# Halves of w_in by model dimension, four early blocks, and batch 1's k and v in halves: one edit to a fused attention and feed-forward kernel

## The chip, the cores and the metric

The kernel runs on one core of a Trainium2 chip. The metric is the time of the whole program on the device in microseconds; runs of one kernel on this chip agree within some tenths of a per cent. One execution was also recorded by the hardware profiler, and all times "at" a point below are counted from the start of that recording. PE is the TensorE (matmul) engine, ACT is ScalarE, DVE is VectorE, POOL is GpSimd and SP is SyncE, which here only issues DMA requests.

## The reference

Linear attention over 8 batches of 8 heads, 576 positions and 64 features, followed by a feed-forward layer with a "snake" activation. Everything is float32 in the reference; the kernel computes its matmuls in bf16.

```python
q_s = softmax(q, axis=features);  k_s = softmax(k, axis=positions)
kv  = einsum('bhsd,bhse->bhde', k_s, v)
x   = einsum('bhsd,bhde->bhse', q_s, kv)      # -> 4608 tokens x 512
h   = x @ w_in                                # 4608 x 2048
g   = h + sin(alpha*h)**2 / (alpha + 1e-9)
out = g @ w_out                               # 4608 x 512
```

## The kernel before

**Tiles.** The tokens are cut into 9 tiles `t` of 512. A batch has 9 blocks of 64 tokens, so tile 0 is the first 8 blocks of batch 0, tile 1 is block 8 of batch 0 and the first 7 blocks of batch 1, and so on. `xT` holds x transposed: 4 chunks of 128 model dimensions (the k steps `ki`) by 4608 tokens.

**The two matmul stages.** For one tile, `mm_h` (L248) makes 16 blocks `ni` of 128 columns of h, each with 4 matmuls, one for each `ki`, accumulated in one PSUM buffer. On each block ACT takes the sine (L254), ACT, POOL or DVE squares it (L256, L258, L260; letters A, P, D in a string say which), and DVE adds the parts to g (`combine`, L264), which frees the block's PSUM buffer. `combine` runs one block behind. The squares live in a pool of 4 `s` buffers. Then `mm_o` (L268) makes the output, 4 row groups `m` by 16 steps over `ni`, and the sums are copied out (L274) and stored (L277). For tile 0 this output stage is `o_quad`, with four accumulators open at once and an order written out by hand: four groups `c` of four w_out rows each, by `m` first or by row first. For later tiles it is `o_stream`, one accumulator after the other.

**Hand-made order.** Every engine runs its instructions in the order in which the code issues them. `take(os, n)` puts the next n output matmuls at that place of PE's order, so attention work of batch 1 is threaded between tile 0's last output matmuls.

**PSUM.** `ps_h` has 4 buffers of one bank; `ps_e` has 2 buffers of two banks, used by the attention steps of batches 0 and 1 and lent to some of the h blocks (`wide`; in the trace these are called `hh`, those in `ps_h` `hp`). Which blocks are lent is decided by `ni % 6`: (2, 3) for tile 0, (4, 5) for tile 1. A new tile of a pool gets the buffer that was released first. After tile 1's h blocks `ps_e` is closed, and `ps_o` (accumulators, called `op`) and `ps_a` take its banks: `ps_o` the first two-bank buffer, `ps_a` the second.

**The head.** Batch 0's q, k, v come in halves; half `ii` holds heads of chunks 2ii and 2ii+1. `kv_mm` (L171) and `kv_norm` (L181, L184) make the block-diagonal `kbd` of a half, `q_transpose_ii` (L200) transposes the normalised q, and `attn_chunk` (L228, `xp`) makes one chunk of x, copied to `xT` (L355, L357, L363). The first two blocks of h do their k steps 0 and 1 ahead of the rest. ACT loads the Sin table (L364) after the last of these copies.

**Requests.** SP asks for q, k, v. POOL asks for w_in (five column ranges, each in two halves by partition) and w_out (four groups of 4 rows): the first eight rows early, the rest by `late`, a table of what is issued after block `ni` of tile 0. `late` also asks for q of batch 1 and, with two small DVE copies as a gate (L90), for k of batch 1. v of batch 1 takes the staging buffer of batch 0's q, which is free after the exp of q's ninth block (block 8).

Of the kernel before, what the change touches and what calls it, by code (L numbers as in the profile page):

```python
# [15 lines left out]
F32 = mybir.dt.float32  # L16
# [7 lines left out]
def kernel(  # L24
# [14 lines left out]
    nc = tc.nc  # L39
# [37 lines left out]
    def src_view(t, b):  # L77
        return t[b].rearrange("(i e) (p j) d -> (e p) i (j d)", e=2, j=J)
# [26 lines left out]
    def load_win(c0, c1):  # L105
        n = slice(c0, c1)
        for x in range(2):
            nc.gpsimd.dma_start(out=win[64 * x:64 * x + 64, :, n], in_=win_v[x][:, :, n])

    def load_wout(c):  # L110
        nc.gpsimd.dma_start(out=wout[:, 4 * c:4 * c + 4, :], in_=wout_v[:, 4 * c:4 * c + 4, :])
# [122 lines left out]
    HP = {}  # L234

    def mm_h(t, ni, wide=None, k0=0, k1=4):

        if ni == 0 and k0 == 0:
            G[t] = gpool.tile([128, nN, MF], BF16, name="g")
        if k0:  # L240
            hp = HP[t, ni]
        elif wide and ni % 6 in ((2, 3) if t == 0 else (4, 5)):
            hp = wide()
        else:
            hp = ps_h.tile([128, MF], F32, name="hp", tag="h")
        HP[t, ni] = hp
        for ki in range(k0, k1):
            nc.tensor.matmul(hp, win[:, ki, ni * 128:(ni + 1) * 128],  # L248
                             xT[:, ki, t * MF:(t + 1) * MF], start=(ki == 0), stop=(ki == 3))
        return hp  # L250
# [70 lines left out]
    for c0, c1 in ((0, 256), (256, 512), (512, 1024), (1024, 1536), (1536, 2048)):  # L321
        load_win(c0, c1)
    for c in range(2):
        load_wout(c)
# [24 lines left out]
    cast_v0(1, 0, 5, ACT_CP)  # L349
    cast_v0(1, 5, 9, DVE_CP)  # L350

# [5 lines left out]
    ACT_CP(xT[:, 1, 0:MF], xp[1])  # L357
    kv_mm(0, 1, ps_e, split=True)
    kv_norm(0, 1, 2)
    xp = [ps_e.tile([128, 2, MF], F32, name="xp", tag="a")[:, 0] for _ in range(2)]  # L360
    for e in range(2):
        attn_chunk(0, 2 + e, 0, 8, xp[e])
        (DVE_CP, ACT_CP)[e](xT[:, 2 + e, 0:MF], xp[e])  # L363
    nc.scalar.activation(zero, zero, AX.Sin)  # L364
    for ki in range(2):
        for ni in range(2):
            mm_h(0, ni, None, ki, ki + 1)

    def h_slot(t, ni, sq, lag, wide=None):
        hp = mm_h(t, ni, wide, 2 if t < 2 and ni < 2 else 0)  # L370
        lag.append((t, ni, hp, sine(t, ni, hp, sq)))
# [5 lines left out]
    def o_quad(t, accs, engs):  # L377

        R = range(4)
        by_m, by_n = [(n, m) for m in R for n in R], [(n, m) for n in R for m in R]  # L380
        orders = [by_m, by_n, by_n, by_m]
        for c in R:
            for n, m in orders[c]:
                mm_o(t, m, 4 * c + n, accs[m])
                if c == 3 and n == 3:
                    evac_o(t, m, accs[m], engs[m])
                yield
# [9 lines left out]
    with ES:  # L397
        def lent():
            return ps_e.tile([128, 2, MF], F32, name="hh", tag="a")[:, 0]

        def load_q8():
            for ii in range(2):
                load0(nc.sync, "q", q, ii, 8, 9)

        def load_q1():
            staged["q", 1] = st = stage.tile([128, 4, J, D], F32, name="st_q", tag="st")
            for ii in range(2):
                DVE_CP(st[:, ii, 0, 0:1], zero)
            for ii in range(2):
                nc.sync.dma_start(out=st[:, ii::2, 0:7].rearrange("p i j d -> p i (j d)"),  # L410
                                  in_=src_view(q, 1)[:, ii::2, 0:7 * D])

        late = {4: load_q8, 6: load_q1, 8: lambda: load_wout(2),
                10: lambda: load_wout(3), 13: lambda: load("k", k, 1, halves=True, gate=DVE_CP)}
# [10 lines left out]
        exp_to(A["qe", 0][:, 8:9], staged["q", 0][:, :, 8:9])  # L425
        for ii in range(2):
            exp_half("q", 1, ii, 7)
        load("v", v, 1, halves=True)
        nc.sync.dma_start(out=q78.rearrange("p i j d -> p i (j d)"), in_=src_view(q, 1)[:, :, 7 * D:J * D])
        load_batch(2)  # L430
        norm_late(0, 8)
        norm_q(1, [GP, V], 7)
        exp_k(1)
# [9 lines left out]
        take(os, 6)  # L443
# [4 lines left out]
        cast_v(1, [ACT_CP, DVE_CP])  # L448
        exp_to(A["qe", 1][:, 7:J], q78)
        take(os, 3)  # L450
        kv_mm(1, 0, ps_e, split=True)
        kv_norm(1, 0, 1)
        take(os, 3)
        kv_mm(1, 1, ps_e, split=True)
        kv_norm(1, 1, 2)
        take(os, 1)

        c0 = J * P
        for ii in range(2):
            xp = ps_e.tile([128, 2, 512], F32, name="xp", tag="a")[:, :, 0:7 * P]  # L460
            for e in range(2):
                attn_chunk(1, 2 * ii + e, 0, 7, xp[:, e])
            (ACT_CP, DVE_CP)[ii](xT[:, 2 * ii:2 * ii + 2, c0:c0 + 7 * P], xp)
            if ii == 0:
                nc.scalar.activation(zero, zero, AX.Sin)
            take(os, 2)
# [5 lines left out]
        for ki in range(2):  # L472
            for ni in range(2):
                mm_h(1, ni, lent, ki, ki + 1)
# [72 lines left out]
    def lent():  # L547
        return ps_o.tile([128, MF], F32, name="op", tag="o")
# [70 lines left out]
```

## Time and profile before

| what | value |
|---|---|
| median of 3 runs | 287.51 us (287.39 to 287.79) |
| span of the profiled execution | 285.8 us; its own time is not given apart from the span |
| PE busy | 272.6 us, 95% of the span |
| ACT, DVE, POOL busy | 226.0, 192.6, 80.6 us |
| granted TensorE clock | 0.999 on the mean |
| first h matmul of tile 0, first output matmul of tile 0 | 14.64 us, 28.42 us |
| first h matmul of tile 1, first output matmul of tile 1 | 46.14 us, 59.95 us |
| batch 1: k halves landed | 37.33 and 39.40 us |
| batch 1: v halves landed | 40.85 and 42.28 us |

The span is from the first to the last instruction; the median of the runs is 1.7 us longer than it. Busy times are unions of an engine's instructions. A matmul of 512 columns is shown as 0.379 us, but a new one starts every 0.216 us, so PE's idle time is read from the starts and not from the ends. In a timeline row the columns are the start, the duration, the engine, the line, the operation, out<-in, the shapes and the count; brackets at the end give the engine's idle time ahead of it and what ended it.

### The profile page before, as it was taken

How to read it: one execution, taken by the hardware profiler on the slowest of the kernel's cores; microseconds unless marked ns; L12 is line 12 of the kernel's file. 1: busy time of each engine (PE TensorE's matmuls, PEld its weight loads, DVE VectorE, ACT ScalarE, POOL GpSimd, SP SyncE). 2: the span in 40 equal slices, each digit the busy share in tenths (PEclk: the TensorE clock that was granted, in tenths of full speed). 3: DMA queues.
4: the chain of work that ended last, by engine and by line, in shares of the span. 5: the costliest groups of instructions: out<-in, count | busy, mean ns of one | idle time of the engine just before them, and what ended most of it. 6: DMA issues, size and time to landing. Idle time of an engine off the chain costs nothing.

```text
span 285.8 us, 4247 instructions
## 1 busy us (share of the span) xinstructions
PE 272.6 (95%) x1541; PEld 130.8 (46%) x1569; DVE 192.6 (67%) x291; ACT 226.0 (79%) x321; POOL 80.6 (28%) x75
## 2 busy tenths in 40 slices
PE   2899999999999999999999999999999999999994
PEld 1444454445454454444544454445444444444443
DVE  4857967999999658766785677667674555555321
ACT  4898748999489999899889988998877777777400
POOL 2869512773477480005300530041000000000000
PEclk9999999999999999999999999999999999999999
DMA  7999999843999984139711990016011111111242
GB/s 261 308 204 243 260 397 407 312 169 78 275 222 412 372 169 105 37 69 406 218 38 39 359 292 20 22 36 155 1 39 37 37 37 39 37 38 41 46 100 73
DMA packets 38581, 45.77 MB, mean 160 GB/s; under 512 B 16528, under 2 KB 22432, under 8 KB 38560
## 3 DMA queue, kind: packets, MB, share of 16 engines
q1 hardware_dynamic: 33376, 40.57, 46.3%
q0 software_dynamic: 4992, 4.79, 9.7%
q8 instruction: 12, 0.20, 0.3%
q10 hardware_dynamic: 192, 0.14, 0.2%
q14 instruction: 9, 0.07, 0.1%
HBM read 36.71 MB, written 9.44 MB: 161 GB/s over the span
## 4 chain that ended last, share of the span: by engine, by line
PE 74%; DVE 9%; DMA 7%; ACT 4%; issue 3%; POOL 2%; SPq 0%; ACTq 0%
PE op L268 33%; PE hp L248 33%; DMA st_v<-in_v_dram 5%; ACT s L254 3%; DVE g L264 2%; POOL s L258 2%; PE kvp L171 2%; DVE qs L150 2%; PE xp L220 2%; DMA st_q<-in_q_dram 1%; PE op L589 1%; PE hh L248 1%; DVE vb L137 1%; DVE qn L152 1%; DVE kbd L184 1%
## 5 line engine op out<-in xcount | busy, mean ns | idle before, releaser
L264 DVE SCALAR_TENSOR_TENSOR g<-s,inva_sb,hp 128x512 bf16<-128x512 f32 x130 | 96.0, 745 | 58.4 <-ACT s L256 54.2
L248 PE MATMUL hp<-xT,win 128*128 128x512 bf16 x512 | 129.0, 379 | 0.5
L268 PE MATMUL op<-wout,g 128*128 128x512 bf16 x479 | 121.9, 379 | 1.2 <-issue 0.6
L254 ACT ACTIVATE s<-hp,alpha_sb 128x512 f32<-128x512 f32 x130 | 87.8, 682 | 25.1 <-PE hp L248 22.6
L248 PEld LDWEIGHTS <-win 128*128 128x128 bf16 x576 | 56.3, 98 | 67.5 <-issue 0.8
L268 PEld LDWEIGHTS <-g 128*128 128x128 bf16 x560 | 54.1, 98 | 61.1 <-issue 0.4
L256 ACT ACTIVATE s<-s 128x512 f32<-128x512 f32 x111 | 69.9, 630 | 3.5
L152 POOL TENSOR_TENSOR qn<-qe,qs 128x1152 bf16<-128x1152 bf16 (+1 forms) x12 | 24.9, 2091 | 78.6 <-DVE qs L146 69.2
L258 POOL TENSOR_TENSOR s<-s 128x512 f32<-128x512 f32 x30 | 33.0, 1111 | 22.3 <-ACT s L254 22.0
L274 DVE COPY o<-op 128x512 f32<-128x512 f32 (+2 forms) x33 | 22.0, 668 | 9.7 <-PE op L268 5.8
L118 ACT ACTIVATE ke<-st_k 128x1152 bf16<-128x1152 f32 x16 | 17.9, 1151 | 5.0 <-DMA st_k<-in_k_dram 5.0
L118 ACT ACTIVATE qe<-st_q 128x1152 bf16<-128x1152 f32 (+3 forms) x18 | 17.7, 1025 | 2.1 <-DMA st_q<-in_q_dram 1.9
L145 DVE TENSOR_REDUCE qs<-qe 128x36 f32<-128x2304 bf16 x5 | 12.8, 2553 | 8.7 <-ACT qe L118 8.6
L268 PE MATMUL hp<-wout,g 128*128 128x512 bf16 x62 | 14.8, 379 | 0.2 <-issue 0.2
L223 DVE CAST xT<-xp 128x512 bf16<-128x512 f32 (+1 forms) x18 | 13.4, 742 | 0.0
L137 POOL CAST vb<-st_v 128x1152 bf16<-128x1152 f32 x10 | 11.3, 1163 | 6.5 <-DMA st_v<-in_v_dram 6.5
L171 PEld LDWEIGHTS <-ke 64*128 64x128 bf16 x288 | 8.4, 93 | 4.9 <-issue 1.9
L171 PE MATMUL kvp<-vb,ke 64*128 64x130 bf16 x288 | 9.9, 216 | 0.7 <-ACT vb L137 0.4
L118 ACT ACT_TABLE_LOAD x7 | 9.0, 1283 | 1.3 <-PEq L603 1.2
L248 PE MATMUL hh<-xT,win 128*128 128x512 bf16 x39 | 9.6, 379 | 0.1
L220 PE MATMUL xp<-qT,kbd 128*128 128x256 bf16 (+1 forms) x40 | 8.2, 286 | 0.4 <-DVE xT L223 0.3
L150 DVE TENSOR_REDUCE qs<-qe 128x16 f32<-128x1024 bf16 (+2 forms) x6 | 7.2, 1197 | 1.8 <-ACT qe L118 1.8
(79 smaller groups left out, 123.1 us busy)
## 6 DMA issues: line engine op xcount, KB each, us to landing
out_dram<-o SPq DMA_DIRECT2D x70, 128.0 KB, 2.3
st_q<-in_q_dram SPq DMA_DIRECT2D x6, 1152.0 KB, 6.7
st_k<-in_k_dram SPq DMA_DIRECT2D x6, 1152.0 KB, 8.9
st_v<-in_v_dram SPq DMA_DIRECT2D x6, 1152.0 KB, 10.2
st_k<-in_k_dram SPq DMA_DIRECT2D x4, 576.0 KB, 7.1
wout<-in_moe_w_out_dram POOLq DMA_DIRECT2D x4, 512.0 KB, 11.7
st_v<-in_v_dram SPq DMA_DIRECT2D x3, 576.0 KB, 9.4
win<-in_moe_w_in_dram POOLq DMA_DIRECT2D x6, 256.0 KB, 7.7
```

What stands on the lines that cost most here:

```text
L118: nc.scalar.activation(dst[:, :, ii * 128:(ii + 1) * 128].rearrange("p j (x d) -> p x j d", x=2), src[:, ii::2], AX.Exp)
L137: engs[ii](vv[:, 2 * ii:2 * ii + 2, :, 0:D], staged["v", b][:, ii::2])
L152: engs[ii % len(engs)].tensor_tensor(qn[:, ii, 0:j1].rearrange("p j (x d) -> p j x d", x=2), qe[:, ii], part.unsqueeze(3).to_broadcast([12 ...
L171: nc.tensor.matmul(kvp[:, e, ii * 130:(ii + 1) * 130], ke[r, j, ii * 128:(ii + 1) * 128], vt[r, j, ii * 130:(ii + 1) * 130], start=(j == 0 ...
L220: nc.tensor.matmul(xp[:, e, 0:n], kt[:, e, ii], qT[:, ii, j0:j1, e * 64:(e + 1) * 64], start=True, stop=True)
L248: nc.tensor.matmul(hp, win[:, ki, ni * 128:(ni + 1) * 128], xT[:, ki, t * MF:(t + 1) * MF], start=(ki == 0), stop=(ki == 3))
L254: nc.scalar.activation(s, hp, AX.Sin, scale=alpha_sb[:, ni:ni + 1])
L256: nc.scalar.activation(s, s, AX.Square)
L258: nc.gpsimd.tensor_tensor(s, s, s, op=ALU.mult)
L264: nc.vector.scalar_tensor_tensor(G[t][:, ni], in0=s, scalar=inva_sb[:, ni:ni + 1], in1=hp, op0=ALU.mult, op1=ALU.add)
L268: nc.tensor.matmul(acc, G[t][:, ni, j * 128:(j + 1) * 128], wout[:, ni, :], start=(ni == 0), stop=(ni == nN - 1))
L274: eng(o[:, cols], acc)
```

## The change

It has these parts:

- **w_in's first columns.** Columns 0 to 511 are asked for in two halves by model dimension (k steps 0-1, then 2-3) and not as two column ranges; the later ranges are 512 columns each as before. The cast of part of v of batch 0 goes from ACT to POOL, between the w_in requests.
- **Four early blocks.** Blocks 0 to 2 of tile 0 do k step 0 ahead of the last two x chunks; block 3 follows behind those, and then all four do k step 1. The Sin table is loaded ahead of this. Both x chunks now share one two-bank buffer.
- **Lent buffers.** The blocks of tile 0 that use `ps_e` are those with `ni % 6` 3 or 5, from block 3 on; in tile 1 those with 0 or 1, where blocks 0 and 1 share one buffer. From tile 2 on the choice is as before.
- **Batch 1.** k and v are asked for together, half by half (k, v, k, v), after block 13 of tile 0, with one DVE copy as a gate. q's ninth block of batch 0 is loaded into `q78` behind batch 1's q. The exps, casts, `kv_mm` and x chunks of batch 1 are issued half by half, and blocks 0 and 1 of tile 1 do k steps 0 and 1 between `kv_mm` of the second half and its x chunks.
- **w_out's last rows.** Rows 12-13 are asked for in `late`, rows 14-15 after the normalisation of batch 1's q. In the last group of `o_quad` rows 12 and 13 go first for all four accumulators, then 14 and 15.

The diff, cut to its core:

```diff
-    def load_win(c0, c1):
-        n = slice(c0, c1)
+    def load_win(c0, c1, k0=0, k1=4):
+        n, kk = slice(c0, c1), slice(k0, k1)
...
+    LENT = {0: (3, 5), 1: (0, 1), 2: (4, 5)}
...
-        elif wide and ni % 6 in ((2, 3) if t == 0 else (4, 5)):
-            hp = wide()
+        elif wide and ni % 6 in LENT[t]:
+            hp = wide(t, ni)
...
-    for c0, c1 in ((0, 256), (256, 512), (512, 1024), (1024, 1536), (1536, 2048)):
-        load_win(c0, c1)
+    load_win(0, 512, 0, 2)
+    load_win(0, 512, 2, 4)
+    load_win(512, 1024)
+    cast_v0(1, 0, 5, GP_CP)
+    for c in range(2, 4):
+        load_win(512 * c, 512 * c + 512)
...
-    cast_v0(1, 0, 5, ACT_CP)
     cast_v0(1, 5, 9, DVE_CP)
+
+    def lent(t, ni):
+        if (t, ni) != (1, 1):
+            HP["pair"] = ps_e.tile([128, 2, MF], F32, name="hh", tag="a")
+        return HP["pair"][:, int((t, ni) == (1, 1))]
...
+    nc.scalar.activation(zero, zero, AX.Sin)
     kv_mm(0, 1, ps_e, split=True)
     kv_norm(0, 1, 2)
-    xp = [ps_e.tile([128, 2, MF], F32, name="xp", tag="a")[:, 0] for _ in range(2)]
+    for ni in range(3):
+        mm_h(0, ni, lent, 0, 1)
+    xp = ps_e.tile([128, 2, MF], F32, name="xp", tag="a")
     for e in range(2):
-        attn_chunk(0, 2 + e, 0, 8, xp[e])
-        (DVE_CP, ACT_CP)[e](xT[:, 2 + e, 0:MF], xp[e])
-    nc.scalar.activation(zero, zero, AX.Sin)
-    for ki in range(2):
-        for ni in range(2):
-            mm_h(0, ni, None, ki, ki + 1)
+        attn_chunk(0, 2 + e, 0, 8, xp[:, e])
+    for e in range(2):
+        (DVE_CP, ACT_CP)[e](xT[:, 2 + e, 0:MF], xp[:, e])
+    mm_h(0, 3, lent, 0, 1)
+    for ni in range(4):
+        mm_h(0, ni, lent, 1, 2)
...
-        orders = [by_m, by_n, by_n, by_m]
+        orders = [by_m, by_n, by_n, by_n[:8] + [(n, m) for m in R for n in (2, 3)]]
...
+            nc.sync.dma_start(out=q78[:, :, 0], in_=src_view(q, 0)[:, :, 8 * D:J * D])
+
+        def load_kv1():
+            for n in "kv":
+                staged[n, 1] = stage.tile([128, 4, J, D], F32, name=f"st_{n}", tag="st")
+            DVE_CP(staged["k", 1][:, 0, 0, 0:1], zero)
+            for ii in range(2):
+                for n, t in (("k", k), ("v", v)):
+                    nc.sync.dma_start(out=staged[n, 1][:, ii::2].rearrange("p i j d -> p i (j d)"),
+                                      in_=src_view(t, 1)[:, ii::2])
-        late = {4: load_q8, 6: load_q1, 8: lambda: load_wout(2),
-                10: lambda: load_wout(3), 13: lambda: load("k", k, 1, halves=True, gate=DVE_CP)}
+        late = {6: load_q1, 8: lambda: load_wout(8, 12), 10: lambda: load_wout(12, 14), 13: load_kv1}
...
-        exp_to(A["qe", 0][:, 8:9], staged["q", 0][:, :, 8:9])
         for ii in range(2):
             exp_half("q", 1, ii, 7)
-        load("v", v, 1, halves=True)
+        exp_to(A["qe", 0][:, 8:9], q78[:, :, 0:1])
...
-        norm_late(0, 8)
         norm_q(1, [GP, V], 7)
-        exp_k(1)
+        norm_late(0, 8)
+        load_wout(14, 16)
...
+        exp_half("k", 1, 0)
+        cast_v1(0, ACT_CP)
+        exp_half("k", 1, 1)
...
-        take(os, 6)
+        take(os, 4)
         xp = ps_e.tile([128, 4, P], F32, name="xp", tag="a")
...
+        kv_mm(1, 0, ps_e, split=True)
+        kv_norm(1, 0, 1)
+        cast_v1(1, DVE_CP)
+        take(os, 4)
+        x_half(0, ACT_CP)
+        exp_to(A["qe", 1][:, 7:J], q78)
+        nc.scalar.activation(zero, zero, AX.Sin)
+        take(os, 2)
+        kv_mm(1, 1, ps_e, split=True)
+        kv_norm(1, 1, 2)
+        for ki in range(2):
+            for ni in range(2):
+                mm_h(1, ni, lent, ki, ki + 1)
+        x_half(1, DVE_CP)
         take(os)
```

`x_half(ii, eng)` makes the two x chunks of a half for 7 blocks of batch 1 and copies them to `xT`, as the loop at L459 did.

## The prediction

> **What bounds the kernel now.** I read the chain that ended last, then TensorE's (PE's) timeline round every edit, then VectorE's (DVE's), then the landings of the requests that move.
>
> ```profile
> PE 74%; DVE 9%; DMA 7%; ACT 4%; issue 3%; POOL 2%; SPq 0%; ACTq 0%
> ```
>
> PE sets the end: sixteen 128x512 matmuls from 46.14 are followed by the next at 49.59, so one costs 0.216 us, and nearly all of the span is such steps. A change is worth what it takes from or adds to PE's idle time; what leaves PE busy at its old place costs nothing.
>
> ```profile
> 11.78 0.60 PE L228 MATMUL hp<-qT,kbd 128*128 128x512 bf16 x2
> 12.39 0.69 PE L171 MATMUL kvp<-vb,ke 64*128 64x130 bf16 x18
> 13.98 0.61 PE L228 MATMUL xp<-qT,kbd 128*128 128x512 bf16 x2 [0.90 <-DVE kbd L184]
> 14.64 1.67 PE L248 MATMUL hp<-xT,win 128*128 128x512 bf16 x7
> 16.15 1.03 PE L248 MATMUL hh<-xT,win 128*128 128x512 bf16 x4
> ```
>
> This is the head (start, duration, count). PE idles 0.90 us for DVE's kbd; from 14.64 it is dense, so the head offers at most that 0.90 and a 0.22 step at 14.43.
>
> ```profile
> 28.42 10.28 PE L268 MATMUL hp<-wout,g 128*128 128x512 bf16 x45
> 38.54 0.95 PE L200 MATMUL tp<-identb,qn 128*128 128x128 bf16 x14
> 40.73 0.28 PE L228 MATMUL xp<-qT,kbd 128*128 128x64 bf16 x4
> 42.09 0.69 PE L171 MATMUL kvp<-vb,ke 64*128 64x130 bf16 x18 [0.44 <-ACT vb L137]
> 42.94 0.59 PE L268 MATMUL hp<-wout,g 128*128 128x512 bf16 x2 [0.16 <-issue]
> 46.14 1.03 PE L248 MATMUL hp<-xT,win 128*128 128x512 bf16 x4
> ```
>
> Here tile 0's output stage starts at 28.42. Its first 46 matmuls (one record is missing) last 10.12 us where 46 x 0.216 = 9.93: 0.19 of waiting is hidden in the group. Batch 1's k and v cost PE 0.44 + 0.16 us of idleness between 41.5 and 43.
>
> ```profile
> 28.55 0.75 DVE L264 SCALAR_TENSOR_TENSOR g<-s,inva_sb,hp 128x512 bf16<-128x512 f32 x1 [0.38 <-POOL s L258]
> 29.54 0.75 DVE L264 SCALAR_TENSOR_TENSOR g<-s,inva_sb,hp 128x512 bf16<-128x512 f32 x1 [0.24 <-POOL s L258]
> 30.33 0.74 DVE L264 SCALAR_TENSOR_TENSOR g<-s,inva_sb,hp 128x512 bf16<-128x512 f32 x1
> 30.98 1.44 DVE L264 SCALAR_TENSOR_TENSOR g<-s,inva_sb,hh 128x512 bf16<-128x512 f32 x2
> ```
>
> These are the `combine` steps of blocks 11, 12, 13 and 14-15 of tile 0, each freeing the PSUM buffer its block was in. The four accumulators of the output stage take over the buffers of the last four blocks in `ps_h`: now blocks 10, 11, 12, 13. PE wants the second accumulator 4 matmuls after 28.42, at 29.28, and block 11's combine ends at 29.30; it wants the third at 30.2 and block 12's ends at 30.29. That is the hidden 0.19.
>
> ```profile
> 58.58 1.39 DVE L264 SCALAR_TENSOR_TENSOR g<-s,inva_sb,hh 128x512 bf16<-128x512 f32 x2
> 59.90 2.15 DVE L264 SCALAR_TENSOR_TENSOR g<-s,inva_sb,hp 128x512 bf16<-128x512 f32 x3
> ```
> ```profile
> 59.95 2.32 PE L268 MATMUL op<-wout,g 128*128 128x512 bf16 x9
> ```
>
> The same handover at the end of tile 1: `ps_o` lies on the first buffer of `ps_e`, last used by block 10 (the first of the two `hh` at 58.58, done 59.31). PE starts at 59.95 without waiting; blocks 12, 13 and 14 are combined from 59.90 on.
>
> **Part 1, the head.** Three k-step-0 matmuls (3 x 0.216 = 0.65 us) move into the idle 13.08 to 13.98. They need xT's first chunk (DVE until 13.11) and the first w_in pair.
>
> ```profile
> L108 POOL DMA_DIRECT2D win<-in_moe_w_in_dram x1: 659/659/659, 8.2 to 8.2; - x1
> DMA to landing us min/median/max: 5.5/5.5/5.5
> ```
>
> This is the pair's second half: issued 8.25, landed 13.75. The changed pair has the same bytes, so 13.80 is one bound for the start; xT's 13.17 is the other. q's ninth block (128 KB, landed 0.46 us behind k at 9.99) leaves the queue ahead, so I take 13.4. Three matmuls to 14.05, two xp (0.43), five more matmuls (1.08) end at 15.56, with one 0.22 step 15.6 to 15.8; from 13.80 it is 15.96 to 16.2. Before, the same eight matmuls ended at 14.64 + 1.73 = 16.37. Lead: 0.2 to 0.8, taken 0.6. Columns 512 to 1024 landed at 17.66 (10.66 + 7.0) and are wanted four half-blocks later, at 17.3 to 17.7: they may eat 0.3 of the lead.
>
> Hidden edits: the cast of v to GpSimd (POOL) takes some 0.65 us (1.16 x 640/1152), ready near 12.05 for kv_mm at 12.39. It stands ahead of four w_in and two w_out issues, queued behind transfers until 17.66 anyway; POOL's first square is wanted at 17.9 and its issues then end near 16.9. Without that cover each late us of the cast delays kv_mm as much. ScalarE (ACT) loses that 0.72 cast; the Sin load comes ahead of xT's last copy, from about 13.4. The load's row takes 1.28 us (15.23) and the next instruction starts 0.01 later: xT's copy then runs 14.9 to 15.5, just before PE wants it. [...]
>
> **Part 2, buffers of tile 0.** Lent blocks become 3, 5, 9, 11, 15, so the last four in `ps_h` are 10, 12, 13, 14 (a pool gives out the buffer released first), and the second accumulator waits for block 12, not 11. Block 12's combine ends at 30.29 now. Its chain (POOL's squares one behind the other, ACT's sines held by four `s` buffers) starts at ACT's first sine, 16.63, held by the Sin load. Then it starts when block 0 is done, 0.64 us after PE's 15.6 to 15.96: up to 0.4 earlier. The second late w_out issue on POOL is halved in descriptors (0.79 to about 0.66, the w_in issues' row): 0.13 more. So the combine ends at 29.75 to 30.2, and the remaining twelve matmuls of the first group end 12 x 0.216 = 2.59 us later, at 32.4 to 32.8. Third and fourth accumulator follow 0.70 us apart, hidden under 0.86 of matmuls. Before, that point was 28.42 + 3.45 + 0.19 = 32.06. The head's lead is gone, and 0.3 to 0.7 more; **+0.5**.
>
> **Part 3, batch 1's k and v.** Asked for together from 30.2 (q's old buffer is free early), they still share the queue with the same bytes: v's halves landed at 40.85 and 42.28, third and fourth; now v's first half is second, at about 39.2. That takes out the 0.60 us of waiting. q's ninth block, now ahead of k, costs that queue the 0.46 us of its old row; the halved w_out request gives as much back. Its exp also holds SyncE until about 34.3, with q78's second part and batch 2 behind it (32.36 before); k and v fill the queue until 42, so nobody waits. In return only 4, not 6, output matmuls cover DVE's three qT copies: transposes at 38.54, last copy ended 40.48, 1.94 later; PE has 0.89 + 0.86 = 1.75 of work, so it waits some 0.3 with the semaphore. The rest is reordered: after each kv_mm, kbd is ready 1.15 us later (43.93 to 45.05), against 4 matmuls, 0.86 plus 0.15 to 0.37 of restart: 0 to 0.2 each. Sum -0.60 + 0.3 + 0.2 x 2 = **+0.1**, between -0.5 (both waits gone, nothing new) and +0.5. The request for w_out's rows 14-15 stands on POOL behind the qn multiply, at about 35.5; nothing queued behind it is wanted before the next sine near 47. Rows 12-15 took 38.60 - 33.72 = 4.9 us once the queue was theirs, so half takes 2.5, plus issue and latency: about 41, wanted near 46. [...]
>
> **Part 4, buffers of tile 1.** Lent blocks become 0, 1, 6, 7, 12, 13. By release order block 12 sits in `ps_e`'s first buffer, so the output stage's first accumulator waits for its combine: 59.90 + 0.73, against PE's 59.95. Relative to PE that chain is unchanged (ACT waits for PE's blocks 11 and 12). The wait is **+0.65**, up to 0.9 if the evacuations and norm_late, which now come later on DVE, push it. Nothing gives it back: DVE's next evacuation (63.83, waiting 0.26 for PE) heads the chain to batch 3's v request at 71.84.
>
> **Sum.** +0.5 + 0.1 + 0.65 = +1.25 us against the profiled span of 285.8; what lies round it (1.7 us to the median 287.51) stays. 287.51 + 1.25 = 288.8, its own range 0.3 - 0.3 + 0.4 to 0.7 + 0.5 + 0.9: 287.9 to 289.6.
>
> **Rivals.** (a) Faster: the buffers bind nothing and PE keeps the head's 0.6 and part 3's 0.6: 287.51 - 1.2 = 286.3. For it: both waits hang on combines that an earlier ACT could advance. Against: block 12's combine would have to end by 29.0, 1.3 us earlier, and POOL is dense from 22.88 on. It decides where that combine ends before the fourth output matmul; chance 0.18. (b) A wash: the lower ends, +0.3, -0.3 and +0.4, with a stronger k and v gain of another 0.2: 287.7; chance 0.14. (c) Rows 14-15 late: if half the rows take 11.9 us like the whole request at 26.66, they land at 47.4 to 48, 1.5 after PE wants them: 288.8 + 1.5 = 290.3. The queue ahead of that request, which is gone here, speaks against; chance 0.07. The forecast has 0.61.
>
> **Numbers.** About 0.2%, 0.57 us, is what a measurement can tell: faster is below 286.9, slower above 288.1. Faster: 0.18 from (a), 0.01 from the forecast's tail. Same: (b) and 0.01. Slower: (c) and the forecast's rest. The range takes the forecast, (b) and the near part of (a): 286.7 to 289.8.
>
> **What would show it.** Right: PE's first L248 near 13.4 and eight matmuls done before 16; a stall of about 0.9 us after four output matmuls near 29, ended by a DVE combine; no wait for vb near 42; a stall of 0.6 before the first `op` of tile 1's output. Wrong: output matmuls dense from the start, or `op` following the last block at once.

## The result and the profile after

The changed kernel takes 290.76 us (median of 4 runs, 290.35 to 291.31) against 287.45 us before: 1.0107 times, 95% interval 1.009 to 1.0125. The direction was forecast, the size was not: 288.8 us was predicted and the range ended at 289.8. The profiled execution has a span of 288.6 us (285.8 before) and a time of its own of 290.35 us, the shortest of the four, so what it shows covers 2.8 of the 3.3 us between the medians. Line numbers after the change are one higher than before (L249 is the h matmul, L269 the output matmul, L255 the sine, L265 `combine`).

The chain that ended last, by engine, in the page of the changed kernel:

```profile
PE 75%; DVE 9%; DMA 6%; POOL 4%; ACT 2%; issue 2%; SPq 0%; ACTq 0%
```

PE still sets the end, so the 2.8 us must be idle time of PE. TensorE's timeline of the changed kernel, round every edit (start, duration, engine, line, operation; in brackets the idle time ahead of it and what ended that):

```profile
13.52 0.81 PE L249 MATMUL hp<-xT,win 128*128 128x512 bf16 x3
14.31 0.60 PE L228 MATMUL xp<-qT,kbd 128*128 128x512 bf16 x2
...
15.83 1.72 PE L249 MATMUL hp<-xT,win 128*128 128x512 bf16 x6
17.39 0.59 PE L249 MATMUL hh<-xT,win 128*128 128x512 bf16 x2
18.35 1.02 PE L249 MATMUL hp<-xT,win 128*128 128x512 bf16 x4 [0.36 <-DMA win<-in_moe_w_in_dram]
...
28.70 1.03 PE L269 MATMUL hp<-wout,g 128*128 128x512 bf16 x4
30.59 9.22 PE L269 MATMUL hp<-wout,g 128*128 128x512 bf16 x42 [0.85 <-DVE g L265]
39.65 0.94 PE L200 MATMUL tp<-identb,qn 128*128 128x128 bf16 x14
...
41.87 0.68 PE L171 MATMUL kvp<-vb,ke 64*128 64x130 bf16 x18
...
44.38 0.69 PE L171 MATMUL kvp<-vb,ke 64*128 64x130 bf16 x18
...
48.09 0.59 PE L249 MATMUL hh<-xT,win 128*128 128x512 bf16 x2
49.84 0.59 PE L249 MATMUL hh<-xT,win 128*128 128x512 bf16 x2 [1.16 <-ACT s L255]
...
63.02 2.32 PE L269 MATMUL op<-wout,g 128*128 128x512 bf16 x10 [0.50 <-DVE g L265]
```

Four places lose time. Block 4 of tile 0 waits for w_in's columns 512 on (18.35). After four output matmuls the second accumulator waits for a combine (30.59). Tile 1's block 1 waits 1.16 us for ACT's sine (49.84), which no step of the prediction had. The first `op` waits for a combine (63.02). In this profile neither `kv_mm` of batch 1 waits (41.87 and 44.38 have no bracket).

The account, from marks that both traces have (us):

| stretch | before | after | difference |
|---|---|---|---|
| start of the span to tile 0's first output matmul | 28.42 | 28.70 | +0.28 |
| from there to batch 1's transposes (46 output matmuls) | 10.12 | 10.95 | +0.83 |
| transposes to tile 1's h, less four early matmuls (4 x 0.216) | 7.60 | 7.58 | -0.02 |
| tile 1's h, 64 matmuls, to the first `op` | 13.81 | 15.79 | +1.98 |
| from there to the end | 225.80 | 225.55 | -0.25 |
| sum | 285.75 | 288.57 | +2.82 |

A step, here and below, is the time from one matmul's start to the next, 0.216 us when nothing waits; the 1.16 and 0.50 us of the brackets are 1.32 and 0.66 us beyond that. They make up the fourth row's 1.98.

The first row is chance as far as these profiles show. The second `kv_mm` of batch 0 started at 12.72 instead of 12.39; `p_before` below, whose head is that of the kernel before, started it at 12.66 and its output at 28.70, as late as the changed kernel. Counted from that `kv_mm`, tile 0's output began after 16.03 us before, 16.04 in `p_before` and 15.98 after the change.

### The profile page after: what moved, and what is told of

Read it like the earlier page. It is cut to its first block, busy times and chain, and to the rows that moved or that the text cites. A ratio compares the mean times of both kernels' runs of the same rounds, so it can differ in the third digit from the quotient of the medians.

```text
span 288.6 us, 4272 instructions
## 1 busy us (share of the span) xinstructions
PE 276.0 (96%) x1569; PEld 130.8 (45%) x1569; DVE 193.4 (67%) x290; ACT 225.9 (78%) x320; POOL 81.2 (28%) x77
## 4 chain that ended last, share of the span: by engine, by line
PE 75%; DVE 9%; DMA 6%; POOL 4%; ACT 2%; issue 2%; SPq 0%; ACTq 0%
PE op L269 34%; PE hp L249 30%; DVE g L265 4%; PE hp L269 4%; DMA win<-in_moe_w_in_dram 3%; DMA st_v<-in_v_dram 2%; ACT s L255 2%; PE kvp L171 2%; POOL s L259 2%; DMA st_k<-in_k_dram 2%; PE xp L220 2%; PE hh L249 1%; PE op L610 1%; DVE vb L137 1%; POOL win L108 1%
## 5 line engine op out<-in xcount | busy, mean ns | idle before, releaser
L265 DVE SCALAR_TENSOR_TENSOR g<-s,inva_sb,hp 128x512 bf16<-128x512 f32 x129 | 95.2, 745 | 57.3 <-ACT s L257 54.2
L249 PE MATMUL hp<-xT,win 128*128 128x512 bf16 x516 | 129.6, 379 | 0.6 <-DMA win<-in_moe_w_in_dram 0.4
L269 PE MATMUL op<-wout,g 128*128 128x512 bf16 x496 | 124.4, 379 | 0.5 <-DVE g L265 0.5
L255 ACT ACTIVATE s<-hp,alpha_sb 128x512 f32<-128x512 f32 x129 | 87.5, 683 | 25.3 <-PE hp L249 24.3
L249 PEld LDWEIGHTS <-win 128*128 128x128 bf16 x576 | 56.0, 98 | 69.5 <-issue 3.2
L269 PEld LDWEIGHTS <-g 128*128 128x128 bf16 x560 | 54.1, 98 | 62.8 <-issue 1.9
L259 POOL TENSOR_TENSOR s<-s 128x512 f32<-128x512 f32 x30 | 32.3, 1089 | 25.5 <-ACT s L255 25.2
L118 ACT ACTIVATE qe<-st_q 128x1152 bf16<-128x1152 f32 (+2 forms) x16 | 17.2, 1115 | 2.3 <-DMA st_q<-in_q_dram 2.1
L269 PE MATMUL hp<-wout,g 128*128 128x512 bf16 x64 | 14.8, 379 | 0.9 <-DVE g L265 0.9
L223 DVE CAST xT<-xp 128x512 bf16<-128x512 f32 (+1 forms) x18 | 13.4, 743 | 0.0
L249 PE MATMUL hh<-xT,win 128*128 128x512 bf16 x44 | 11.4, 379 | 1.2 <-ACT s L255 1.2
L265 DVE SCALAR_TENSOR_TENSOR g<-s,inva_sb,hh 128x512 bf16<-128x512 f32 x11 | 8.0, 742 | 2.1 <-POOL s L259 2.0
L255 ACT ACTIVATE s<-hh,alpha_sb 128x512 f32<-128x512 f32 x11 | 7.4, 682 | 2.0 <-PE hh L249 1.9
```

The lines of the kernel that those rows point to most:

```text
L118: nc.scalar.activation(dst[:, :, ii * 128:(ii + 1) * 128].rearrange("p j (x d) -> p x j d", x=2), src[:, ii::2], AX.Exp)
L223: eng(xT[:, 2 * ii:2 * ii + 2, c0:c0 + n], xp[:, :, 0:n])
L249: nc.tensor.matmul(hp, win[:, ki, ni * 128:(ni + 1) * 128], xT[:, ki, t * MF:(t + 1) * MF], start=(ki == 0), stop=(ki == 3))
L255: nc.scalar.activation(s, hp, AX.Sin, scale=alpha_sb[:, ni:ni + 1])
L259: nc.gpsimd.tensor_tensor(s, s, s, op=ALU.mult)
L265: nc.vector.scalar_tensor_tensor(G[t][:, ni], in0=s, scalar=inva_sb[:, ni:ni + 1], in1=hp, op0=ALU.mult, op1=ALU.add)
```

## The experiments

The first three are the changed kernel with one handover mended each; the fourth is the second with one cast moved back. All later ones use the normalised q of batches 2 to 7 untransposed, by plain copies of the same bytes, so that they have a before and an after of their own (`p_before`, `p_after`); their line numbers are six or more lower than those of the changed kernel. The table gives the stretches of each profile; ratios are to the kernel before, run on the same chip beside it. Four chips were used (e1 to e4; `p_before` to `p_m1`; `p_h1` to `p_f3`; `p_m4` and `p_f4`), so across these groups the ratios compare and the medians do not.

| kernel | median us | ratio, 95% interval | start to first sine | sine to tile 0's output | output to transposes | transposes to tile 1's first sine | sine to `op` | `op` to end |
|---|---|---|---|---|---|---|---|---|
| before | 287.45 | - | 16.63 | 11.79 | 10.12 | 9.16 | 12.26 | 225.80 |
| after | 290.76 | 1.0107 (1.009-1.0125) | 16.73 | 11.97 | 10.95 | 9.46 | 13.92 | 225.55 |
| e1_pair | 290.07 | 1.0076 (1.0059-1.0093) | 17.24 | 11.81 | 10.96 | 9.89 | 12.96 | 225.51 |
| e2_t0lent | 291.35 | 1.0121 (1.0102-1.014) | 16.68 | 11.97 | 10.08 | 10.62 | 14.74 | 225.53 |
| e3_t1lent | 290.19 | 1.0078 (1.0061-1.0096) | 16.61 | 12.07 | 10.95 | 9.46 | 13.25 | 225.53 |
| e4_t0lent_cast | 290.68 | 1.0099 (1.0076-1.0123) | 17.34 | 11.81 | 10.10 | 9.13 | 14.74 | 226.07 |
| p_before | 287.80 | 1.0013 (0.9991-1.0035) | 16.90 | 11.80 | 10.12 | 8.88 | 12.26 | 225.79 |
| p_after | 290.57 | 1.009 (1.0066-1.0114) | 16.81 | 11.83 | 10.95 | 9.80 | 13.91 | 225.53 |
| p_f1 | 289.07 | 1.0031 (1.0009-1.0053) | 17.11 | 11.81 | 10.10 | 10.70 | 12.36 | 225.54 |
| p_m1 | 288.50 | 1.0024 (1.0008-1.004) | 17.06 | 11.91 | 10.08 | 11.01 | 12.36 | 225.53 |
| p_h1 | 288.65 | 1.001 (0.9997-1.0022) | 17.57 | 12.03 | 10.09 | 9.45 | 12.34 | 225.79 |
| p_m2_q8 | 289.18 | 1.0026 (1.0013-1.0039) | 17.52 | 11.80 | 10.10 | 9.57 | 12.36 | 225.53 |
| p_m3_rows | 288.88 | 1.0018 (1.0005-1.003) | 17.42 | 11.81 | 10.12 | 9.84 | 12.35 | 225.55 |
| p_f3 | 289.22 | 1.0029 (1.0017-1.0042) | 17.90 | 11.91 | 10.11 | 9.89 | 12.35 | 225.53 |
| p_m4 | 287.69 | 0.9996 (0.9979-1.0012) | 16.77 | 11.80 | 10.12 | 9.31 | 12.26 | 225.53 |
| p_f4 | 289.18 | 1.005 (1.0031-1.0069) | 19.42 | 11.86 | 10.12 | 9.63 | 12.22 | 225.52 |

The "start to first sine" column holds chance as well: batch 0's first half of q, whose request no kernel changes, landed between 4.33 and 5.26 us. The later columns repeat from profile to profile within some 0.1 us wherever no DMA is waited for.

**e1_pair.** Both early blocks of tile 1 are finished before the first sine is issued.

```diff
+        two = [mm_h(1, ni, lent, 2) for ni in range(2)]
         for ni in range(nN):
-            h_slot(1, ni, SQ[ni], lag, lent)
+            if ni < 2:
+                lag.append((1, ni, two[ni], sine(1, ni, two[ni], SQ[ni])))
+            else:
+                h_slot(1, ni, SQ[ni], lag, lent)
             flush(lag, 1)
```

> The changed kernel, with both early blocks of tile 1 finished by PE before the first sine is issued; nothing else differs. Theory: the changed kernel's 3.3 us are three PE waits for buffers (1.0 us at the second accumulator of tile 0, 1.3 us at block 1 of tile 1, whose matmuls are ordered behind ACT's sine of block 0 since both sit in one tile of ps_e, and 0.65 us at the first accumulator of tile 1) and a head that brings nothing. Then the 1.3 us wait at block 1 disappears, the first sine starts 0.4 us later against PE, and the time falls by 1.0 to 1.4 us, to 289.4 to 289.8 (ratio to the kernel before 1.007 to 1.008). Rival: ACT, not the shared tile, sets the pace there, so PE waits the same 1.3 us a few blocks later and the time stays at 290.8 (1.011).

The wait is gone, but the first sine comes 0.43 us later, the two matmuls of block 1 that now precede it (9.46 to 9.89). TensorE's timeline of this kernel:

```profile
48.45 1.03 PE L249 MATMUL hh<-xT,win 128*128 128x512 bf16 x4
49.31 3.62 PE L249 MATMUL hp<-xT,win 128*128 128x512 bf16 x16
...
62.86 1.46 PE L269 MATMUL op<-wout,g 128*128 128x512 bf16 x6 [0.90 <-DVE g L265]
```

From tile 1's first sine to `op` it takes 12.96 us instead of 13.92; with the 0.43 given back that is 0.53 net, and the ratio is the theory's (1.0076; 1.007 to 1.008 expected). The bracket at `op` grew from 0.50 to 0.90. So the 1.16 us bracket was the shared buffer; but PE still waits for a combine at tile 1's end, so mending the one wait moved part of it there.

**e2_t0lent.** Tile 0 lends blocks 3, 4, 8, 9, 14, 15, so that its last four blocks in `ps_h` are 10 to 13 as before.

```diff
-    LENT = {0: (3, 5), 1: (0, 1), 2: (4, 5)}
+    LENT = {0: (3, 4, 8, 9, 14, 15), 1: (0, 1, 6, 7, 12, 13), 2: (4, 5, 10, 11)}
...
-        elif wide and ni % 6 in LENT[t]:
+        elif wide and ni in LENT[t]:
```

> The changed kernel with blocks 3, 4, 8, 9, 14, 15 of tile 0 lent (in place of 3, 5, 9, 11, 15), so that the output stage's accumulators follow blocks 10, 11, 12, 13 as in the kernel before. Theory: the wait after the fourth output matmul falls from 1.0 to 0.1 to 0.3 us and the time by 0.7 to 0.9 us, to 289.9 to 290.1 (1.0085 to 1.009). Rival: the lost time is upstream, in w_in's later landing and POOL's chain, and a later accumulator waits instead: 290.5 to 290.8 (1.0105 to 1.0115).

```profile
28.64 4.63 PE L269 MATMUL hp<-wout,g 128*128 128x512 bf16 x20
...
44.62 0.69 PE L171 MATMUL kvp<-vb,ke 64*128 64x130 bf16 x18 [1.09 <-DVE vb L450]
...
50.08 0.59 PE L249 MATMUL hh<-xT,win 128*128 128x512 bf16 x2 [1.16 <-ACT s L255]
...
64.08 1.24 PE L269 MATMUL op<-wout,g 128*128 128x512 bf16 x5 [1.32 <-DVE g L265]
```

Tile 0's output is dense again, 10.08 us: the mended handover is what cost 0.83. The kernel is no faster all the same (291.35, where 289.9 to 290.1 was expected), for two reasons that the rows name. v's second half landed at 43.69, so its `kv_mm` waits 1.09. And `op` waits 1.32 instead of 0.50: six lent blocks instead of five in tile 0 swap the two buffers of `ps_e`, so that `op`'s buffer was last used by block 13, whose combine ends at 64.03, and not by block 12 (63.20). An even or odd number of lent blocks in one tile decided what the next tile's end waits for; e4, with the same sets, has the same 14.74.

**e3_t1lent.** Tile 1 alone lends 0, 1, 5, 6, 10, 11 (the same edit, tile 0's set as changed).

> The changed kernel with blocks 0, 1, 5, 6, 10, 11 of tile 1 lent (in place of 0, 1, 6, 7, 12, 13), so that the accumulators of tile 1's output follow block 10. Theory: the 0.66 us wait of the first output matmul of tile 1 disappears and the time falls by 0.6 us to 290.1 (1.009). Rival: DVE's late combines are wanted by the same output matmuls anyway, or batch 3's request moves it back: 290.8 (1.0115).

```profile
49.83 0.59 PE L249 MATMUL hh<-xT,win 128*128 128x512 bf16 x2 [1.16 <-ACT s L255]
...
62.35 1.89 PE L269 MATMUL op<-wout,g 128*128 128x512 bf16 x8
```

`op` waits for nothing, and the stretch falls by 0.67 (13.92 to 13.25): Part 4's wait is the lent set's and is worth what it was priced at.

**e4_t0lent_cast.** e2 with the cast of batch 0's v back on ACT.

```diff
-    cast_v0(1, 0, 5, GP_CP)
...
+    cast_v0(1, 0, 5, ACT_CP)
     cast_v0(1, 5, 9, DVE_CP)
```

> The kernel of e2 with the cast of the first part of v's second half back on ACT, as before the change. Theory: the cast on POOL holds up the descriptors of the w_in requests behind it; w_in's columns 512 to 1023 land near 17.6 and not 18.2, PE's wait of 0.5 us before block 4 of tile 0 disappears, and the time is 0.3 to 0.6 us below e2's (1.007). Rival: the landing is late because of the new shape of the first four w_in requests (2 k steps by 512 columns); the wait stays and the time is e2's or, with ACT later, 0.2 above.

```profile
14.28 0.81 PE L249 MATMUL hp<-xT,win 128*128 128x512 bf16 x3 [1.16 <-DMA win<-in_moe_w_in_dram]
```

w_in's columns 512 on landed at 16.71 and 17.98 (e2: 16.86 and 18.15; after: 16.94 and 18.21; before: 16.39 and 17.66), so most of their lateness is not POOL's cast. Here the gap in w_in's arrivals lay ahead of the first pair (batch 0's v at 11.49, the pair at 13.50 and 14.15), and PE waited 1.16 us for that instead of 0.36 at block 4. The median is 0.67 us below e2's, as the theory had it, but the profile gives no support to its reason: what is shorter is the stretch to tile 1's first sine (9.13 instead of 10.62), where batch 1's v landed at 42.21 and its `kv_mm` does not wait, and where the sine itself starts 0.32 us sooner behind its matmul (last section).

**p_before and p_after** are the two kernels with the plain copies.

> The kernel before with the transposing DMAs of q in batches 2 to 7 replaced by plain copies of the same bytes from the same queue (q of these batches is used untransposed). It is the base for the kernels below, which have the same copies. They start after 68 us, behind everything that the change touches. Theory and rival alike: PE is dense there, so the time is that of the kernel before, 287.0 to 287.6 (0.998 to 1.000), and PE's waits up to 60 us are those of the kernel before.

> The changed kernel with the same plain copies. Theory and rival alike: 3.0 to 3.5 us above p_before (1.0105 to 1.012), with the three waits at the second accumulator of tile 0 (1.0 us), block 1 of tile 1 (1.3) and the first accumulator of tile 1 (0.65).

They stand 0.0077 apart in ratio, 2.77 us, a little below the 3.0 to 3.5 expected; the copies themselves are worth 1.0013 (0.9991 to 1.0035). Tile 1's stretch, 13.91, and tile 0's, 10.95, are those of the change. This pair gives the account a second time. In the rows of the first it reads -0.06, +0.83, +0.59, +1.98 and -0.26, in sum 3.08: the second and fourth rows repeat to 0.01, the first and third do not. `p_before` waited 0.16 us for v's first half, not 0.44, and in `p_after` v's second half landed at 43.73 (after: 42.54), so that PE waited for it:

```profile
42.65 0.81 PE L263 MATMUL hp<-wout,g 128*128 128x512 bf16 x3 [0.16 <-issue]
...
44.66 0.69 PE L171 MATMUL kvp<-vb,ke 64*128 64x130 bf16 x18 [0.28 <-DVE vb L444]
```

**p_f1 and p_m1.** p_f1 is the change with all three handovers mended (e1, e2 and e3 together). p_m1 is the same with the head of the kernel before, so batch 1's part alone.

> The kernel of p_after with all three handovers mended: lent blocks 3, 4, 8, 9, 14, 15 in tile 0 and 0, 1, 5, 6, 10, 11 in tile 1, and both early blocks of tile 1 finished before the first sine. Theory (the 3.3 us are the three waits): they come off together, since each alone only moved part of its time into the next handover; the time is 0.3 to 0.9 us above p_before (1.001 to 1.003). Rival (the time is lost to later landings of w_in and of batch 1's v, and waits refill): 1.7 to 2.5 us above p_before (1.006 to 1.009).

> The kernel of p_before with the batch 1 part alone: k and v half by half, q's ninth block late, w_out's last rows late, blocks 0 and 1 of tile 1 early in one lent buffer and both finished before the first sine, lent blocks of tile 1 0, 1, 5, 6, 10, 11; head and tile 0 as before. Theory: PE's waits for batch 1 (0.6 us near 42) go, and as much comes in between kv_mm, kbd and x; within 0.4 us of p_before (0.9985 to 1.0015). Rival: the requests in halves bring a gain that the changed kernel hides, 0.6 to 1.0 us below p_before (0.997); or v's second half lands after it is wanted, 0.8 above (1.003).

Mending takes p_f1 from 290.57 to 289.07, half of what the change cost. Both handover columns are nearly back (10.10 and 12.36); what remains stands between batch 1's transposes and tile 1's first sine, 10.70 and 11.01 against 8.88. In p_m1's profiled execution v's second half landed at 44.30 (42.30 in p_before):

```profile
45.23 0.69 PE L171 MATMUL kvp<-vb,ke 64*128 64x130 bf16 x18 [1.38 <-DVE vb L438]
```

That execution took 289.74, the longest of the 12, 1.24 over their median, so a wait of this size most likely belongs to some executions and not to all.

**p_m2_q8 and p_m3_rows** change one request each in p_m1: q's ninth block after block 4, and w_out's rows 12 to 15 in one request after block 10.

```diff
-            nc.sync.dma_start(out=q78[:, :, 0], in_=src_view(q, 0)[:, :, 8 * D:J * D])
+        late = {4: lambda: nc.sync.dma_start(out=q78[:, :, 0], in_=src_view(q, 0)[:, :, 8 * D:J * D]),
```
```diff
-        late = {6: load_q1, 8: lambda: load_wout(8, 12), 10: lambda: load_wout(12, 14), 13: load_kv1}
+        late = {6: load_q1, 8: lambda: load_wout(8, 12), 10: lambda: load_wout(12, 16), 13: load_kv1}
...
-        load_wout(14, 16)
```

> As p_m1 (batch 1's part alone), but the request for q's ninth block of batch 0 goes out after block 4 of tile 0, as in the kernel before, and not behind batch 1's q. Normalised q of batches 2 to 7 untransposed as in p_before. Theory A (rows 14-15 of w_out, requested at 36.1, share the transfers with v's second half): only that block's 0.46 us leaves the queue, so v's second half lands near 43.8 instead of 44.30, its kv_mm still waits about 1.1 us, time 288.1 to 288.5. Theory B (that block ahead of k is the cause): v's second half lands near 42.5, no wait over 0.3, time about 287.6.

> As p_m1 (batch 1's part alone), but rows 12 to 15 of w_out are asked for together after block 10, as in the kernel before; the output order of the last group stays as changed. Normalised q of batches 2 to 7 untransposed as in p_before. Theory A (rows 14-15 share the transfers with v's second half): it has the kernel before's 42.3 plus 0.46 for q's ninth block, 42.8 at most instead of 44.30; kv_mm of the second half waits less than 0.4 (1.55 in p_m1), and the time falls by 0.5 to 1.0 to 287.5 to 288.0. Theory B (the order k, v, k, v or q's ninth block): landing 43.8 or later, 288.5 as p_m1.

In p_m3_rows v's second half landed at 43.43, where 42.8 at most was expected, but the wait is gone:

```profile
44.36 0.69 PE L171 MATMUL kvp<-vb,ke 64*128 64x130 bf16 x18
```

In p_m2_q8 it is gone too: v's second half landed at 40.81, where 43.8 was expected. So neither cause is singled out: each request moved brings v's second half forward in its profile. In time they gain nothing that the intervals separate (1.0026 and 1.0018 against 1.0024): the late v of p_m1's profile does not set its median. And 0.7 us and more remain before the first sine (9.57 and 9.84 against 8.88).

**p_h1, the head alone**, with the kernel before's batch-1 part and tile 0's lent set of e2.

> The head part alone: w_in's halves by model dimension, the cast of v on GpSimd, four early blocks and the early Sin load, with the kernel before's batch-1 part, its request order and its tile-1 buffers; tile 0 lends blocks 3, 4, 8, 9, 14 and 15, so that the first output group has no accumulator that waits for block 12. The normalised q of batches 2 to 7 is used without its transposition (plain copies of the same bytes). Theory A (the head's lead is lost, since columns 512 to 1023 land at 18.0 to 18.5 instead of 17.66 and block 4 waits for them): nothing is gained; the two parts' costs add, so head = p_f1 - p_m1 = 0.57 us above p_before's 287.8: 288.1 to 288.4. Theory B (the head gains its lead once the buffers are mended, and all of p_f1's remaining cost is batch 1's): 287.0 to 287.4.

1.001 against p_before's 1.0013: the head alone is worth nothing that these intervals show. From the first `kv_mm` to the first sine it took 6.40 us against 6.65 in p_before, and from there to tile 0's output 12.03 against 11.80, with the same wait for w_in at block 4: the lead is gained and given back.

**p_f3** is p_f1 with both request changes.

> p_f1 (the whole change with its three handovers mended) with both request changes: q's ninth block asked for after block 4 and rows 12 to 15 of w_out together after block 10. Normalised q of batches 2 to 7 untransposed as in p_before. Theory A (p_f1's remaining 1.2 us is the late second half of v, 0.91, and what follows from it): 288.0 to 288.3, kv_mm of the second half waits less than 0.3. Theory B (the rest lies in the head and in tile 1's chain of sine, square and combine): 288.7 to 289.1, a wait of about 0.9 stays at block 4 of tile 1. If head and batch 1 both gained what they set out to, it would be below p_before's 287.8.

Not 288.0 to 288.3 but 289.22, on a chip on which the kernel before took 288.22. `kv_mm` no longer waits, yet the time is p_f1's; a wait of 0.69 us at block 6 of tile 1 is left, the pair's buffer again:

```profile
53.53 1.02 PE L243 MATMUL hh<-xT,win 128*128 128x512 bf16 x4 [0.69 <-DVE g L259]
```

Block 6 takes the buffer that blocks 0 and 1 shared, free only when block 1 is combined, at 53.48.

**p_m4 and p_f4** leave the early blocks of tile 1 out. p_m4 is p_m1 with both request changes, tile 1's blocks 0 and 1 after the last output matmul in `ps_h`, and the kernel before's lent set of tile 1; p_f4 adds the changed head.

```diff
-        for ki in range(2):
-            for ni in range(2):
-                mm_h(1, ni, lent, ki, ki + 1)
+        take(os, 4)
         x_half(1, DVE_CP)
```

> Batch 1's part alone with k and v still half by half, q's ninth block asked for after block 4, rows 12 to 15 of w_out together after block 10, and without early blocks of tile 1: blocks 0 and 1 start after the last output matmul in ps_h, tile 1 lends blocks 4, 5, 10 and 11 as in the kernel before, and four output matmuls stand where the early blocks stood. Normalised q of batches 2 to 7 untransposed as in p_before. Theory A (the early blocks are what batch 1's part still costs, because they share one tile and both must be finished before the first sine, two matmuls or 0.43 us later): from batch 1's transposes to tile 1's first sine 9.0 to 9.2 us instead of 9.57 in p_m2_q8 (8.88 in p_before), the profiled span below 286.5, time within 0.3 us of p_before's. Theory B (the half-by-half order itself costs it): 9.5 or more, time as p_m2_q8 and p_m3_rows, 0.5 to 0.8 us above p_before's.

> As p_m4, with the changed head of p_h1 in front (and its buffers of tile 0: blocks 3, 4, 8, 9, 14 and 15). Normalised q of batches 2 to 7 untransposed as in p_before. Theory A (head and halves are both worth about nothing once no handover waits): within 0.3 us of p_before's; the stretch from the first sine of tile 0 to its output stays 11.8 to 12.0. Theory B (the head's earlier start pays when batch 1's part costs nothing): 0.4 us or more below p_before's, faster than the kernel before.

p_m4 is level with the kernel before: 0.9996 (0.9979 to 1.0012), and its tile 1 is dense.

```profile
46.26 3.79 PE L243 MATMUL hp<-xT,win 128*128 128x512 bf16 x16
...
60.24 2.11 PE L263 MATMUL op<-wout,g 128*128 128x512 bf16 x9
```

The stretch to the first sine fell to 9.31, not to 9.0 to 9.2, but the time met the expectation. So the half-by-half order of k and v costs nothing that can be seen, and what was left of batch 1's part, some 0.6 to 0.9 us in the medians (0.0022 to 0.003 in ratio; the intervals just touch), went with its two early blocks and their lent set, which were taken out together. The profiles show part of it: from batch 1's transposes to the end it takes 247.46 and 247.74 us in p_m2_q8 and p_m3_rows, 247.10 here, and with the changed head 247.77 in p_f3, 247.37 in p_f4. In the medians with the changed head the gain does not show (p_f3 1.0029, p_f4 1.005, overlapping intervals). p_m4 is also the best of the variants; none is faster than the kernel before.

p_f4 adds 1.49 us to p_m4 on the same chip, where neither expectation allowed for a loss, and p_h1 had shown none for the same head. Its profiled execution (290.56, one of three of 12 above 290.4) shows the changed head at its worst:

```profile
15.14 0.81 PE L243 MATMUL hp<-xT,win 128*128 128x512 bf16 x3 [2.03 <-DMA win<-in_moe_w_in_dram]
```

The first w_in pair landed at 14.36 and 15.01. In the kernel before, PE wants that pair at 14.64 and it had landed by 13.75; the changed head wants it right after the second `kv_mm`, near 13.1. The head has exchanged a slack of 0.9 us for none, and the arrival is not steady: in the kernels with these requests the pair's second half landed between 13.38 and 15.01. PE waited for that pair in seven of the ten profiles with the changed head, from 0.38 us (e3) to these 2.03; the profile of the changed kernel itself is one of the three without such a wait. Another 0.32 of p_f4's loss, in this profile, lies at tile 1's first sine (9.63 against 9.31; last section). What places the gap in w_in's arrivals is open, and so is what the other nine runs of p_f4 lost.

## Why the prediction was right or wrong

**Direction and one term: right; another by chance.** Every sign listed for "Right" came: the first h matmul at 13.52 and eight done at 15.83, a stall of 0.85 near 30, no wait for vb, a stall of 0.50 before `op`. The forecast missed all the same, because it left out a wait that none of these signs stands for (the term that was missing, below). Part 4's wait was put at 0.65 us and measured 0.66 (e3 removes it). Part 3's +0.1 measured -0.02 here, with no wait for vb, but +0.59 in `p_after` against `p_before`, where vb was waited for: the sum holds, at best, when v's second half lands by the time it is wanted, and that varied. Rival (c) is false: rows 14-15 landed at 43.30, not near 41, but were wanted at 46.

**Part 1, where the lead went.** It began as worked out: the first h matmul at 13.52 (13.4 predicted), and the eight early ones done at 15.83, where before they were done at 16.37. What failed in it is "xT's copy then runs 14.9 to 15.5". ScalarE's timeline of the changed kernel:

```profile
13.91 1.28 ACT L367 ACT_TABLE_LOAD   x1
15.20 0.20 ACT L367 ACTIVATE zero<-zero 128x1 f32<-128x1 f32 x1
15.68 0.59 ACT L376 CAST xT<-xp 128x512 bf16<-128x512 f32 x1 [0.28 <-DVE xT L376]
16.73 0.69 ACT L255 ACTIVATE s<-hp,alpha_sb 128x512 f32<-128x512 f32 x1 [0.46 <-PE hp L249]
```

The load began 0.5 later than taken, behind a copy that began at 13.30. It showed 1.28 us, and the next instruction began 0.01 us after its end, as in the kernel before (1.28 us from 15.23, the next at 16.52). Then the copy waited 0.28 us for DVE's copy of the other chunk. Both chunks now share one buffer; in the kernel before, with a buffer for each, the two copies overlapped (14.41 to 15.10 on DVE, from 14.62 on ACT). ACT's copy ran at 15.68, 0.27 us of PE's time were lost for it, and the first sine came at 16.73, not "up to 0.4 earlier" than 16.63. Block 4's wait for w_in took a further 0.52 in steps, where 0.3 had been allowed. The lead of 0.54 became a lag of 0.28 at the output stage. Of both figures 0.33 is the later start of this profile's second `kv_mm`: counted from there a lead of 0.87 became one of 0.05. Either way 0.8 us were lost, and the head brought nothing. Two smaller sizes were off as well: POOL's cast took 0.83 us, not 0.65, which delayed nothing, and the halved w_out request took 0.76 to issue, not 0.66.

**Part 2, mis-sized by that.** The mechanism held. VectorE's timeline of the changed kernel, combines of blocks 11 and 12:

```profile
28.80 0.75 DVE L265 SCALAR_TENSOR_TENSOR g<-s,inva_sb,hh 128x512 bf16<-128x512 f32 x1 [0.37 <-POOL s L259]
29.79 0.75 DVE L265 SCALAR_TENSOR_TENSOR g<-s,inva_sb,hp 128x512 bf16<-128x512 f32 x1 [0.24 <-POOL s L259]
```

Block 12's combine ends at 30.53 and PE resumes at 30.59. The rule of the sum, that end plus 2.59 us, gives 33.12, and the group ended at 33.18. But the end had been taken as 29.75 to 30.2, from a chain that starts earlier. It started 0.10 later instead and was 0.14 longer than before. The term is +1.12, not +0.5 (0.3 to 0.7), and 0.33 of it is this profile's later start. e2 shows that the lent set brings the wait: without it the 46 matmuls take 10.08 us.

**The term that was missing.** The text on the change says that blocks 0 and 1 of tile 1 share one buffer; the prediction gave this no price and no reason for none. That is the step of the prediction that failed most: its sum of +0.5, +0.1 and +0.65 takes tile 1's h stage as dense. ScalarE's timeline of the changed kernel has the cause:

```profile
49.10 0.69 ACT L255 ACTIVATE s<-hh,alpha_sb 128x512 f32<-128x512 f32 x1 [1.09 <-PE hh L249]
50.47 0.69 ACT L255 ACTIVATE s<-hh,alpha_sb 128x512 f32<-128x512 f32 x1 [0.68 <-PE hh L249]
```

PE's matmuls of block 1 follow the sine of block 0 in program order and write the same tile, in its other bank. They started at 49.84, just when that sine ended (49.10 + 0.69 = 49.79). PE lost 1.32 us, and the second sine came 1.37 us after the first, not 0.58 as in the kernel before. There the same two matmuls follow the same sine in program order too, but write a buffer of their own, and PE does not wait:

```profile
46.14 3.62 PE L248 MATMUL hp<-xT,win 128*128 128x512 bf16 x16
```

This is the largest single term of the change. Some 0.32 of it is the sine's late start (last section): in e4, where the sine is prompt, the wait is 0.84 instead of 1.16. e1 mends it by order alone, for 0.43 us of later start; p_m4 mends it by leaving the early blocks out.

**"Nothing gives it back."** Nearly so: 0.25 us came back after the first `op`. All kernels but one with the changed batch-1 part need 225.51 to 225.55 us from there, e4 226.07, and those with the old one 225.79 or 225.80. The cause was not sought.

**The sum.** +1.11 -0.02 +1.32 +0.66 -0.25 = 2.82 us against a forecast of 1.25. Of the miss of 1.57, 1.32 is the term that was left out and 0.61 is Part 2's size, with 0.33 of chance in it; Part 3 and the end gave some back. The medians stand 3.31 us apart, 0.5 more than this profile shows; p_after's profile, close to its median, has 3.08, with the wait for v in it. Two slips in the working change nothing: 43.93 to 45.05 is 1.12 and not 1.15, and the low end of the range takes -0.3 for Part 3, which had itself said -0.5.

## What to carry to other kernels

When two pieces of work come to share one tile, price every engine that touches the tile: work on one half may wait for another engine's reading of the other (1.16 us here), and the order in which the code issues them decides it (in e1 the wait is gone). A handover by "the buffer released first" depends on how many buffers were taken before it, so a changed set in one tile must be followed into the next one (in e2 the wait at `op` went from 0.50 to 1.32 us); and where a stage's length is the chain of sine, square and combine, mending one of its waits can move part of the time to the next handover (in e1 from 0.50 to 0.90 us). Starting work early on data that lands at an unsteady time gives up slack (0.9 us here, with arrivals from 13.38 to 15.01), and its price is the late arrival, not the usual one (2.03 us in p_f4, none in the changed kernel's profile). One profile holds chance: the rows that a second pair of kernels repeats are the ones to build on.

## What the runs showed of the hardware that was not expected

**After a wait for w_in the matmul clock was halved.** In p_f4 TensorE worked for 1.2 us from 11.9 and then waited until 15.14. The view by windows of that kernel (window, length, busy time of each engine, then the granted clock, the DMA share and GB/s):

```profile
14.00:16.00 2.00, 0.86 (x4) 0.42 (x5) 0.00 (x0) 0.86 (x2) 1.24 (x3) 1.00 1.22 198
16.00:18.00 2.00, 2.00 (x7) 0.78 (x6) 0.69 (x1) 0.59 (x1) 1.48 (x2) 0.56 1.25 206
18.00:20.00 2.00, 2.00 (x7) 0.73 (x6) 0.00 (x0) 0.58 (x1) 0.00 (x0) 0.59 1.24 204
20.00:22.00 2.00, 2.00 (x11) 0.88 (x9) 1.55 (x3) 1.97 (x5) 1.18 (x2) 1.00 1.24 205
```

The granted clock was 0.56 and 0.59 in two windows, and a 512-column matmul took some 0.427 us a step from 16.6 to 19.6; the first six matmuls behind the wait, from 15.14 to 16.22, still came 0.216 us apart. The wait ahead of it was 2.03 us. In the other nine profiles with the changed head, where PE waited 1.18 us at most for the same pair, the mean clock is 0.999 or 1.000. The other two executions of p_f4 above 290.4 us have a mean clock like this one's (0.993 and 0.994, this one 0.994; the nine below have 0.998 to 1.000). The slow stretch here is some 3.4 us long, from 16.2 to 19.6. No run shows what brought it on or what ended it: two of the twelve executions of `p_before`, whose head is that of the kernel before, have a mean clock of 0.994 as well.

**The first sine of tile 1 started 0.42 us after its block's last matmul** (48.09 + 0.59 = 48.68, sine at 49.10). In the kernel before it was 0.10: the sixth matmul from 46.14 ended at 46.14 + 5 x 0.216 + 0.38 = 47.60, the sine began at 47.70. The chain that ended last calls 0.37 of it "issue". e2 and e4 differ in nothing but the engine that casts part of batch 0's v, some 36 us earlier: with the cast on POOL (e2) the sine came after 0.42 us, with the cast on ACT (e4) after 0.10 (47.69 + 0.59 = 48.28, sine at 48.38). It is not the cast's place alone: p_h1, with the cast on POOL and the old batch-1 part, has 0.10. What it is stays open.
